# The overflow branch ahead of the last two adds, and the router of blocks 1 to 3 six slots later: fused attention, MLP and top-2 experts on one core

## The chip, the core and the metric

The kernel runs on one core of one Trainium2 chip. TensorE (PE) multiplies matrices and loads its weights on a parallel track (PEld in the profile); VectorE (DVE), ScalarE (ACT) and GpSimd (POOL) do elementwise work, and SyncE (SP) issues transfers. Each engine runs its own queue of instructions in order and waits on semaphores for the others. The metric is the device time of one execution in microseconds (us): a median of 935.31 us over 3 runs before the change (934.85 to 935.39).

## The reference

Three stages, float32 in and out, 2304 tokens of 512 numbers:

```python
scores = where(0 <= i - j < 64, q @ k.T / 8, -1e9)        # 4 sequences x 8 heads x 576 x 64
x = softmax(scores) @ v                                   # heads side by side: 2304 x 512
h = x @ w_in                                              # 512 -> 2048
x = (h * sigmoid(1.702 * h)) @ w_out                      # 2048 -> 512
noisy = x @ w_gate + log1p(exp(x @ w_noise)) * noise      # 8 experts
top2, weights = the two largest of noisy, softmax over the two
out[token] += weight * (relu(x[token] @ w1[e]) @ w2[e])   # for each of its two experts e
```

## The kernel before

Precision: each float32 operand is held as two float16 parts, and each product is three matmuls (high by high, high by low, low by high). So an elementwise result leaves PSUM (TensorE's accumulator memory) as a high part and a low part, made on ACT, DVE and POOL.

Tokens go in 18 tiles of 128 rows, three tiles to a block, blocks 0 to 5. Attention is done tile by tile. The dense MLP is done block by block in 28 slots: 16 slots of its first product (`s1mm`, line 665, twelve matmuls of 384 columns each) and 12 of its second (`s2mm`, line 700, twelve matmuls of 512 columns each, four slots for each tile). After each first product, ACT takes a tanh (line 670), DVE multiplies (line 673, which also frees the PSUM buffer; there are two buffers `h` and two `y`), ACT rounds to the high part (line 676) and POOL subtracts for the low part (line 679). While block c goes through its MLP, the attention of block c+1 runs between the slots: scores on PE (line 486), mask and maximum on DVE (552, 554), exponentials on ACT (560), normalisation on DVE (564 to 570), split on ACT and POOL (578, 581), a transposing transfer issued by SP (586), and the product with v on PE (line 621).

The router picks the experts of a block. Its inputs are the block's MLP rows `R`, transposed by a transfer (`x2t`) and multiplied by the gate weights (`logits`, lines 748 to 751). Nine pieces follow, `route_a` to `route_i`, some 45 small DVE instructions of 3 to 48 columns, a few on ACT, and three small matmuls (`route_g`, lines 823 to 825) that count how many earlier tokens chose each expert. `route_e` (789 to 799) finds the two best experts, `route_f` (804 to 817) makes one-hot masks, `route_h` (833 to 843) the weights, `route_i` (850 to 865) the slot of each token in its expert's list. Then six scatters (`scatter`, line 877, indirect transfers issued by POOL) write token numbers and weights into those lists in DRAM (`xmeta`). The router of block c runs during the MLP of block c+1; that of block 5 runs during the first expert's work.

Each expert's list has 640 places, five row blocks of 128: `gather` fetches rows, `e_stage1` (line 922) and `e_stage2` (line 929) do the two products, and `fin` (lines 948 to 955) scales the rows by their weights on DVE (line 949) and adds them into `out` with an indirect, accumulating transfer issued by POOL (line 952). Empty places carry weight 0 and an output row of their own past the real rows: `NDUMMY` = 128 such rows, shared by all row blocks. What 640 places can't hold is computed by an overflow loop (`overflow_loop`, line 968 on) that goes over all experts and all rows when there is an overflow, and zero times otherwise. Each engine loads the loop's count from memory (`TENSOR_LOAD cti`) and branches.

The order of work: up to the start of block 2's MLP it is a written list (`SEQ`). From there `tasks` holds (time, function) pairs, where time counts slots; before each slot's own matmuls every task that is due is issued. On DVE, ACT, POOL and SP the instructions stand in the order in which they are issued; PE's order is made from it by a scheduler, which can move a group of matmuls past its neighbours. The times of the router, with t0 = 28 (c + 1), the start of the next block's MLP:

```python
for fn, dt, dl in ((route_a, 5, 3.1), ..., (route_e, 10, 3.5), (route_f, 11, 3.6),
                   (route_g, 13, 5), (route_h, 13, 5.2), (route_i, 14, 5.1)):
    at(t0 + (dl if last else dt + ...), fn, c)
at(t0 + (5.4 if last else (15 if c else ...) + 2 * j + a), scatter, c, j, a)
```

`dl` holds for block 5 alone. So `route_e` to `route_i` of blocks 1 to 3 stand in slots 10 to 14, inside the next block's first product; those of block 0 are in `SEQ`.

Of the kernel before, what the change touches and what calls it, by code (L numbers as in the profile page):

```python
# [8 lines left out]
F32 = mybir.dt.float32  # L9
F16 = mybir.dt.float16  # L10
BF16 = mybir.dt.bfloat16
I32 = mybir.dt.int32
# [3 lines left out]
ALU = mybir.AluOpType  # L16
# [6 lines left out]
E, FE = 8, 1024  # L23
NTILE = 18
NCH = 6
CAP = 640
CAPA = 384
MR = 16
NDUMMY = 128
FS = 16  # L30
SL = 28
ET = mybir.EngineType
# [65 lines left out]
def fused_kernel(ctx, tc, q, k, v, w_in, w_out, w_gate, w_noise, noise, w1, w2, out, cap=CAP):  # L98
# [10 lines left out]
    def T(pool, shape, dt, tag, bufs=None):  # L109
        return pool.tile(shape, dt, name=tag, tag=tag, bufs=bufs)  # L110
# [49 lines left out]
    WL = {}  # L160
    WS = {}
    wide = w_in.dtype == I64

    def w_tile(key):
        a = wp.tile([128, 2, 4096], F16, name="w", tag="w", bufs=4)
        WS[key] = (a.rearrange("p s (c n) -> p s c n", c=4), a.rearrange("p s (c n) -> p s c n", c=8))
# [478 lines left out]
    def flush():  # L645
        todo = list(pend)
        pend.clear()
        for fn in todo:
            fn()

    def later(fn):
        pend.append(fn)
# [229 lines left out]
        SC.append(s)  # L882


    XE, ME, OP, ADD = {}, {}, {}, {}
    p2 = {}

    def open2():
# [27 lines left out]
    def moe1(w, x, n, f, o, pool_p):  # L916
        HB[0] += 1
        hp = T(pm, [128, n], F32, "y" if HB[0] > 12 and HB[0] % 2 else "h", 2)
        m = 0
        for d in range(4):  # L920
            for a, s in ((0, 0), (0, 4), (1, 0)):
                pe.matmul(hp, w[:, a, d, 128 * f:128 * f + 128], x[:, s + d, :], start=m == 0, stop=m == 11)  # L922
                m += 1
        later(lambda: relu_split(o, hp))

    def moe2(w, lhs, half, yp):
        for f in range(4 * half, 4 * half + 4):
            for a, s in ((0, 0), (0, 1), (1, 0)):
                pe.matmul(yp, lhs[:, f, a, :], w[:, s, f, :], start=f == 0 and a + s == 0, stop=f == 7 and a == 1)  # L929
# [5 lines left out]
    def e_stage2(e, t, half):  # L935
        part, tt = (0, t) if t < 3 else (1, t - 3)
        g = (gA if part == 0 else gB)[:, :, :, 128 * tt:128 * tt + 128]
        if half == 0:
            OP[e, t] = T(p2["p"], [128, 512], F32, "o", 3)
        yp = OP[e, t]  # L940
        moe2(WS["e2", e][1], g, half, yp)
        if half == 1:
            m = ME[e, part]
            wcol = m[:, tt, e:e + 1].bitcast(F32)
            ids = m[:, tt, 8:9]
            ot = T(p2["s"], [128, 512], F32, "ot", 4)

            def fin():
                dve.tensor_scalar(ot, yp, wcol, None, op0=ALU.mult)  # L949
                if ADD.setdefault(e, []):  # L950
                    pool.memset(C["sp"], 0.0)
                s = pool.indirect_dma_start(out=out, out_offset=bass.IndirectOffsetOnAxis(ap=ids, axis=0),  # L952
                                            in_=ot, in_offset=None, compute_op=ALU.add)
                for o in ADD[e]:
                    tc.declare_no_dep(s.ins, o.ins, reason="an expert takes a token once")
                ADD[e].append(s)
            later(fin)


    def overflow():  # L960
# [7 lines left out]
    def overflow_loop():  # L968
        n = nc.values_load(C["cti"][0:1, 0:1], min_val=0, max_val=E)  # L969
        s2 = p2["s"]  # L970
        with tc.For_i(0, n, 1) as e:
            pool.dma_start(ovd.rearrange("e p t -> p e t"), C["ov"])
            ovc = T(s2, [128, NTILE], F32, "ovc", 1)
            pool.dma_start(ovc, ovd[bass.ds(e, 1)].rearrange("o p t -> p (o t)"))
            for kind in ("e1", "e2"):
                w_tile((kind, "ov"))
                src = (w1 if kind == "e1" else w2)[bass.ds(e, 1)].rearrange("o (c p) f -> p (o c) f", p=128)
                for p in range(4):
                    st = T(mp, [128, 1024], I32, "wst", 3)
                    c = 4 if kind == "e1" else 2  # L980
                    pool.dma_start(st.bitcast(F32).rearrange("p (c n) -> p c n", c=c),
                                   src[:, :, 256 * p:256 * p + 256] if kind == "e1" else src[:, 2 * p:2 * p + 2, :])
                    WL[(kind, "ov"), p] = st
                    wcast((kind, "ov"), p)
            for i in range(NTILE):
                x = T(s2, [128, 8, 128], F16, "xo", 2)
                sp.dma_start_transpose(out=x, in_=x2buf[i + 1])
                ho = T(s2, [128, 8, 2, 128], F16, "ho", 2)
                for f in range(8):
                    moe1(WS["e1", "ov"][0], x, 128, f, ho[:, f], pm)  # L990
                    flush()
                yp = T(p2["p"], [128, 512], F32, "o", 3)
                for half in range(2):
                    moe2(WS["e2", "ov"][1], ho, half, yp)
                ot = T(s2, [128, 512], F32, "ot", 4)
                dve.tensor_scalar(ot, yp, ovc[:, i:i + 1], None, op0=ALU.mult)
                pool.indirect_dma_start(out=out, out_offset=bass.IndirectOffsetOnAxis(ap=C["idm"][:, i, 0:1], axis=0),
                                        in_=ot, in_offset=None, compute_op=ALU.add)


    tasks = []
# [1 line left out]
    def at(t, fn, *a):  # L1003
        tasks.append((t, len(tasks), fn, a))
# [27 lines left out]
    for c in range(NCH):  # L1032
        last = c == NCH - 1
        for j in range(3):
            d = 4 * j if c else 8 + 0.1 * j + P["r0"]
            l = (7 if last and j == 2 else 8) if c else P["l0"]
            at(SL * c + FS + d + (5 if c else P["x0"]), x2t, 3 * c + j)
            at(SL * c + FS + d + l, logits, 3 * c + j)
        t0 = SL * (c + 1)
        for fn, dt, dl in ((route_a, 5, 3.1), (route_b, 6, 3.2), (route_c, 7, 3.3), (route_d, 8, 3.4), (route_e, 10, 3.5),  # L1040
                           (route_f, 11, 3.6), (route_g, 13, 5), (route_h, 13, 5.2), (route_i, 14, 5.1)):
            if last and fn == route_i:
                dl = 5.3
            at(t0 + (dl if last else dt + (0 if c else P["l0"] - 8 + P["r0"])), fn, c)
        for j in range(3):
            for a in range(2):
                at(t0 + (5.4 if last else (15 if c else 17 + P["r0"]) + 2 * j + a), scatter, c, j, a)
    for n in range(4):
        at(2 * SL + 9 + 2 * n, zero_out, n)

# [93 lines left out]
    while ti < len(tasks):  # L1144
        tasks[ti][2](*tasks[ti][3])
        ti += 1
    overflow_loop()


# [27 lines left out]
```

## Time and profile before

| | |
|---|---|
| median of 3 runs | 935.31 us |
| the profiled execution | 933.35 us, of which its span is 931.6 us |
| PE busy | 878.2 us, 94% of the span |
| DVE, ACT, POOL busy | 483.9, 388.2, 372.0 us |
| mean granted TensorE clock | 0.978 of full speed |
| dense MLP of blocks 2 to 5 | 208 to 496 us |
| experts | 497 to 916 us |
| last matmul to end of span | 15.7 us |

The span is from the first to the last instruction. "PE busy" counts matmuls in flight. A row of the timeline has the start in us, the duration (of all that are merged in it), engine, line of the kernel, operation, what it writes and reads, the count (x), and in brackets how long the engine was idle just before and which engine's result, or which transfer, ended that. An engine's name with a q is its sequencer, which handles semaphores, branches and transfer issues and is not counted as busy.

### The profile page before, as it was taken

The numbers are of one execution on the slowest core, as the hardware profiler recorded it, in microseconds if no ns is written. First come the engines' busy times: TensorE is split into PE (matmuls) and PEld (weight loads), VectorE is DVE, ScalarE is ACT, GpSimd is POOL, SyncE is SP. The second block draws the span as 40 slices with busy tenths as digits, with TensorE's granted clock in tenths as the row PEclk, the third lists the DMA queues.
The fourth block names the chain that finished last, engine by engine and source line by source line (L and its number), as shares of the span: only waits on it lengthen the run. The fifth ranks groups of instructions, "written<-read, shape, count | busy, mean of one in ns | idle before, by whom it ended". The sixth has DMA issues, their size and how long they took to land. (4 is left out here: it accounts for less than half of the span.)

```text
span 931.6 us, 16441 instructions
## 1 busy us (share of the span) xinstructions
PE 878.2 (94%) x6355; PEld 502.9 (54%) x6355; DVE 483.9 (52%) x1022; ACT 388.2 (42%) x884; POOL 372.0 (40%) x380
## 2 busy tenths in 40 slices
PE   5898998999899899999999999999999999999993
PEld 4664554545445545545544556674655656474651
DVE  8999976654825734742744522553443525252210
ACT  5888664636426524732633312351322315050200
POOL 2567674826625443551451621432313140323021
PEclk9889999999999999999999999999999999999997
DMA  9899999747887477521248674995866849392112
GB/s 249 215 229 197 232 214 186 129 80 184 238 148 136 81 137 137 81 60 46 91 128 202 142 148 80 231 262 120 192 149 132 209 99 242 48 259 36 23 25 36
DMA packets 255124, 135.90 MB, mean 146 GB/s; under 512 B 207456, under 2 KB 231680, under 8 KB 255040
## 3 DMA queue, kind: packets, MB, share of 16 engines
q1 hardware_dynamic: 218336, 74.28, 41.0%
q0 software_dynamic: 12160, 28.00, 14.3%
q10 hardware_dynamic: 24544, 32.51, 11.4%
q8 instruction: 52, 0.85, 0.4%
q14 instruction: 32, 0.26, 0.1%
HBM read 76.46 MB, written 21.07 MB: 105 GB/s over the span
## 5 line engine op out<-in xcount | busy, mean ns | idle before, releaser
L929 PE MATMUL o<-w,gb 128*128 128x512 f16 x960 | 210.1, 379 | 0.9 <-DVE gb L912 0.7
L700 PE MATMUL y<-w,gb 128*128 128x512 f16 x816 | 185.1, 380 | 0.0
L922 PEld LDWEIGHTS <-w 128*128 128x128 f16 x1536 | 150.1, 98 | 60.5
L952 POOL DMA_INDIRECT out_dram<-ot,me x40 | 69.5, 1739 | 234.7 <-DVE ot L949 228.0
L665 PEld LDWEIGHTS <-w 128*128 128x128 f16 x1152 | 111.5, 99 | 94.1 <-issue 23.1
L929 PEld LDWEIGHTS <-gb 128*128 128x128 f16 x960 | 93.4, 98 | 112.0 <-DVE gb L912 1.6
L665 PE MATMUL h<-xT,w 128*128 128x384 f16 x744 | 137.4, 338 | 14.7 <-DVE gf L673 12.1
L700 PEld LDWEIGHTS <-gb 128*128 128x128 f16 x864 | 82.3, 98 | 94.9 <-issue 1.2
L922 PE MATMUL h<-xe,w 128*128 128x384 f16 (+1 forms) x840 | 126.5, 302 | 0.0
L679 POOL TENSOR_TENSOR gb<-gf,gb 128x384 f16<-128x384 f32 x96 | 91.1, 954 | 81.5 <-ACT gb L676 81.3
L949 DVE TENSOR_SCALAR ot<-o,me 128x512 f32<-128x512 f32 x40 | 30.0, 751 | 144.3 <-PE o L929 122.1
L922 PE MATMUL y<-xe,w 128*128 128x256 f16 (+1 forms) x696 | 102.1, 297 | 0.0
L911 ACT ACTIVATE gb<-y 128x256 f16<-128x256 f32 (+1 forms) x58 | 24.9, 429 | 182.5 <-PE y L922 182.4
L265 DVE SCALAR_TENSOR_TENSOR w<-wst,w 128x1024 f16<-128x1024 f32 x64 | 78.5, 1227 | 40.2 <-ACT w L246 40.2
L246 ACT ACTIVATE w<-wst 128x1024 f16<-128x1024 f32 x64 | 67.5, 1056 | 30.6 <-DVE w L265 17.2
L906 POOL DMA_INDIRECT xg<-x2buf,me x40 | 42.8, 1069 | 72.3 <-DMA me<-xmeta 39.2
L665 PE MATMUL y<-xT,w 128*128 128x384 f16 x408 | 70.0, 326 | 1.5 <-DVE gf L673 1.5
L676 ACT ACTIVATE gb<-gf 128x384 f16<-128x384 f32 x96 | 49.2, 517 | 41.6 <-DVE gf L673 41.6
L560 ACT ACTIVATE sm<-sm,st 128x128 f32<-128x128 f32 x144 | 55.9, 391 | 11.0 <-DVE st L554 10.9
L911 ACT ACTIVATE gb<-h 128x384 f16<-128x384 f32 (+1 forms) x70 | 30.6, 438 | 68.1 <-PE h L922 67.2
L912 DVE SCALAR_TENSOR_TENSOR gb<-h,gb 128x384 f16<-128x384 f32 (+1 forms) x70 | 34.6, 494 | 41.6 <-ACT gb L911 41.6
L877 POOL DMA_INDIRECT xmeta<-rm,slot x36 | 38.5, 1070 | 39.9 <-DVE ov L865 31.5
(167 smaller groups left out, 936.7 us busy)
## 6 DMA issues: line engine op xcount, KB each, us to landing
wst<-in_moe_w_dram ACTq DMA_DIRECT2D x62, 512.0 KB, 4.1
wst<-in_moe_w_in_dram SPq DMA_DIRECT2D x16, 512.0 KB, 4.8
wst<-in_moe_w_out_dram SPq DMA_DIRECT2D x16, 512.0 KB, 4.3
vv<-in_v_dram SPq DMA_DIRECT2D x18, 256.0 KB, 4.8
x2buf<-R SPq DMA_DIRECT2D x18, 256.0 KB, 2.4
kq<-in_k_dram SPq DMA_DIRECT2D x16, 256.0 KB, 4.5
kq<-in_q_dram SPq DMA_DIRECT2D x16, 256.0 KB, 4.5
out_dram<-z POOLq DMA_DIRECT2D x3, 1280.0 KB, 6.2
```

The lines of the kernel that those rows point to most:

```text
L246: act.activation(o[:, 0], i, AF.Copy, scale=s)
L265: dve.scalar_tensor_tensor(o[:, 1], i, s, o[:, 0], op0=ALU.mult, op1=ALU.subtract)
L560: act.activation(sm[:, u, :], sm[:, u, :], AF.Exp, bias=st[:, 0, u:u + 1], accum_out=st[:, 1, u:u + 1])
L665: pe.matmul(hp, w[:, a, d, fs], xt[:, x + d, :], start=n == 0, stop=n == 11)
L676: act.activation(g1[:, f, 0], GF[c, f], AF.Copy)
L679: pool.tensor_tensor(g1[:, f, 1], GF.pop((c, f)), g1[:, f, 0], op=ALU.subtract)
L700: pe.matmul(YP[i], g1[:, f, a, 128 * j:128 * j + 128], w[:, s, f % 8, :], start=f == 0 and a + s == 0, stop=f == 15 and a == 1)
L906: pool.indirect_dma_start(out=xg, out_offset=None, in_=src, in_offset=bass.IndirectOffsetOnAxis(ap=ME[e, part][:, t, 9:10], axis=0))
L911: act.activation(o[:, 0], hp, AF.Relu)
L922: pe.matmul(hp, w[:, a, d, 128 * f:128 * f + 128], x[:, s + d, :], start=m == 0, stop=m == 11)
L929: pe.matmul(yp, lhs[:, f, a, :], w[:, s, f, :], start=f == 0 and a + s == 0, stop=f == 7 and a == 1)
L952: s = pool.indirect_dma_start(out=out, out_offset=bass.IndirectOffsetOnAxis(ap=ids, axis=0), in_=ot, in_offset=None, compute_op=ALU.add)
```

## The change

Four edits:

1. `route_e` to `route_i` and the scatters of blocks 1 to 3 come six slots later: slots 16 to 20 and 21 to 26, inside the second product of the next block's MLP. `route_a` to `route_d` keep slots 5 to 8. Block 4 keeps its times; block 0 is in the written list.
2. For block 5, the third tile's `logits` and all of the router and the scatters come one slot later.
3. The overflow loop stands inside a branch (`tc.If(n != 0)`), and the `fin` of the last expert's row blocks 3 and 4 (two DVE multiplications and two adds of POOL) is issued after that branch, where before all `fin` came ahead of the loop. The loop's result tiles are others (`r`, `xg`), since those of the experts are still held.
4. `NDUMMY` is 1024, so that the empty places of an expert's last two row blocks have output rows of their own. `out` grows by 896 rows, which the kernel neither clears nor returns.

```diff
-NDUMMY = 128
+NDUMMY = 1024
...
-            later(fin)
+            if e == E - 1 and t > 2:
+                LAST.append(fin)
+            else:
+                later(fin)
...
-        with tc.For_i(0, n, 1) as e:
-            pool.dma_start(ovd.rearrange("e p t -> p e t"), C["ov"])
+        with tc.If(n != 0, preferred_fallthrough_block=False):
+            with tc.For_i(0, n, 1) as e:
+                pool.dma_start(ovd.rearrange("e p t -> p e t"), C["ov"])
...
-                yp = T(p2["p"], [128, 512], F32, "o", 3)
+                    yp = T(pm, [128, 512], F32, "r", 1)
...
-                ot = T(s2, [128, 512], F32, "ot", 4)
+                    ot = T(s2, [128, 512], F32, "xg", 4)
...
-            l = (7 if last and j == 2 else 8) if c else P["l0"]
+            l = 8 if c else P["l0"]
...
-        for fn, dt, dl in ((route_a, 5, 3.1), (route_b, 6, 3.2), (route_c, 7, 3.3), (route_d, 8, 3.4), (route_e, 10, 3.5),
-                           (route_f, 11, 3.6), (route_g, 13, 5), (route_h, 13, 5.2), (route_i, 14, 5.1)):
+        late = 0 if last or c == NCH - 2 else 6
+        for fn, dt, dl in ((route_a, 5, 4.1), (route_b, 6, 4.2), (route_c, 7, 4.3), (route_d, 8, 4.4),
+                           (route_e, 10 + late, 4.5), (route_f, 11 + late, 4.6), (route_g, 13 + late, 6),
+                           (route_h, 13 + late, 6.2), (route_i, 14 + late, 6.3)):
...
-                at(t0 + (5.4 if last else (15 if c else 17 + P["r0"]) + 2 * j + a), scatter, c, j, a)
+                at(t0 + (6.4 if last else (15 + late if c else 17 + P["r0"]) + 2 * j + a), scatter, c, j, a)
...
     overflow_loop()
+    for fn in LAST:
+        fn()
```

How the instructions stand, in three places. First DVE during the MLP of block 3, where the weights of block 2's tokens are made (`route_h`). Before:

```order
L570 TENSOR_TENSOR sm<-sm,st 128x512
L833 TENSOR_SCALAR r_wv<-r_wv 128x3
L834 TENSOR_SCALAR r_wv<-r_wv 128x3
L835 RECIPROCAL r_wv<-r_wv 128x3
L836 TENSOR_TENSOR r_wv<-r_wv 128x3
L838 TENSOR_TENSOR r_G<-r_oh_4415,r_wv 128x24
L839 TENSOR_TENSOR r_tg<-r_oh_4416,r_wv 128x24
L840 TENSOR_TENSOR r_G<-r_G,r_tg 128x24
L842 COPY rm<-r_G 128x3x8
L843 COPY rm<-idm 128x3x8
L673 SCALAR_TENSOR_TENSOR gf<-gf,h 128x384
```

The same nine instructions on DVE in the changed kernel:

```order
L554 TENSOR_REDUCE st<-sm 128x4
L636 SCALAR_TENSOR_TENSOR xT<-x,xT 128x4x128
L833 TENSOR_SCALAR r_wv<-r_wv 128x3
L834 TENSOR_SCALAR r_wv<-r_wv 128x3
L835 RECIPROCAL r_wv<-r_wv 128x3
L836 TENSOR_TENSOR r_wv<-r_wv 128x3
L838 TENSOR_TENSOR r_G<-r_oh_4612,r_wv 128x24
L839 TENSOR_TENSOR r_tg<-r_oh_4613,r_wv 128x24
L840 TENSOR_TENSOR r_G<-r_G,r_tg 128x24
L842 COPY rm<-r_G 128x3x8
L843 COPY rm<-idm 128x3x8
L419 COPY qk_4660<-qk_4660 128x8x64
```

The multiplication of line 673, which frees a PSUM buffer of the first product, stood behind them; now the last of these multiplications is past, and what follows is a copy for the attention (line 419).

Second, PE at the three counting matmuls of block 1's router (`route_g`), as a difference: taken out between the scores (486) and a first product (665),

```order
 L486 LDWEIGHTS qT
 L486 MATMUL s<-kT,qT 64x64
-L823 LDWEIGHTS u
-L823 MATMUL r<-r_M,u 128x24
-L824 LDWEIGHTS u
-L824 MATMUL r<-r_mc,u 128x24
-L825 LDWEIGHTS u
-L825 MATMUL r<-r_mc,u 128x8
 L665 LDWEIGHTS w
 L665 MATMUL h<-xT,w 128x384
```

and now between second products (line 700), so that PE meets their wait there.

Third, POOL at the end of the program; `me_9583` are row blocks 0 to 2 of the last expert, `me_9601` row blocks 3 and 4. Before:

```order
L952 DMA out_dram<-ot,me_9583 2432x512
L951 MEMSET sp 1x1
L952 DMA out_dram<-ot,me_9601 2432x512
L951 MEMSET sp 1x1
L952 DMA out_dram<-ot,me_9601 2432x512
L969 TENSOR_LOAD cti
L971 COMPARE_AND_BRANCH
L971 ISA
L971 UNCONDITIONAL_BRANCH
```

In the changed kernel, up to the branch that skips the loop:

```order
L952 DMA out_dram<-ot,me_9583 3328x512
L972 TENSOR_LOAD cti
L974 COMPARE_AND_BRANCH
L974 ISA
L974 UNCONDITIONAL_BRANCH
```

and behind the loop:

```order
L951 MEMSET sp 1x1
L952 DMA out_dram<-ot,me_9601 3328x512
L951 MEMSET sp 1x1
L952 DMA out_dram<-ot,me_9601 3328x512
L1179 UNCONDITIONAL_BRANCH
L1179 ISA
```

The `ISA` instruction of line 971 (now 974) is the one that the profile calls INC_SWDGE_SEM: on the path that skips the loop, POOL first waits until all its earlier transfers have landed, and then sets the semaphores of its transfers to the values that they would have after the loop. Before, this path ends in a block in which every engine waits for all 25 semaphores, twelve instructions on each, and then in the closing barrier (line 1173). In the changed kernel the path leads to the two adds; behind them SP alone waits for the semaphores, and the closing barrier follows.

## Rows read from the trace of the kernel before

**Rows 1.** The page: span.

```profile
span 931.6 us, 16441 instructions
```

**Rows 2.** PE's waits, 225 to 400 us: us in total, times, longest.

```profile
PE h L665 <- DVE gf L673: 7.3, 4, 2.2
PE r L824 <- DVE r_mc L816: 1.1, 2, 0.8
PE r L823 <- DVE r_M L812: 0.7, 1, 0.7
```

**Rows 3.** Timeline, block 2: start us, us, engine, line, work [idle before, releaser].

```profile
244.64 0.55 DVE L673 SCALAR_TENSOR_TENSOR gf<-gf,h 128x384 f32<-128x384 f32 x1
245.24 3.47 PE L665 MATMUL h<-xT,w 128*128 128x384 f16 x12 [2.08 <-DVE gf L673]
...
251.62 1.70 DVE L564 TENSOR_SCALAR st<-st 128x4 f32<-128x4 f32 x1
```

**Rows 4.** Timeline, block 3, DVE and PE.

```profile
308.63 0.69 DVE L789 TENSOR_TENSOR r_ln<-r_ln,r_d 128x24 f32<-128x24 f32 x1
...
317.13 0.88 DVE L833 TENSOR_SCALAR r_wv<-r_wv 128x3 f32<-128x3 f32 x1
...
319.98 0.55 DVE L673 SCALAR_TENSOR_TENSOR gf<-gf,h 128x384 f32<-128x384 f32 x1
...
320.58 2.11 PE L665 MATMUL h<-xT,w 128*128 128x384 f16 x12 [1.86 <-DVE gf L673]
...
323.33 0.19 DVE L865 SCALAR_TENSOR_TENSOR ov<-r_rs,r_G 128x24 f32<-128x24 f32 x1
```

**Rows 5.** Timeline, block 4, DVE and PE.

```profile
386.19 0.69 DVE L789 TENSOR_TENSOR r_ln<-r_ln,r_d 128x24 f32<-128x24 f32 x1
...
388.45 0.55 DVE L673 SCALAR_TENSOR_TENSOR gf<-gf,h 128x384 f32<-128x384 f32 x1
...
389.05 1.98 PE L665 MATMUL h<-xT,w 128*128 128x384 f16 x6 [2.17 <-DVE gf L673]
```

**Rows 6.** Windows: stretch, us, busy us of engines, PEclk (granted clock), DMA share.

```profile
248.00:284.00 36.00, 36.00 (x286) 17.40 (x285) 12.24 (x24) 12.51 (x35) 16.22 (x14) 0.98 0.75 146
245.80:249.30 3.50, 3.50 (x13) 1.54 (x11) 2.57 (x11) 1.83 (x7) 1.85 (x2) 0.51 1.09 222
389.10:392.60 3.50, 3.50 (x15) 1.59 (x14) 2.91 (x11) 1.94 (x7) 0.91 (x1) 0.51 0.12 28
```

**Rows 7.** Timeline of PE after the end of the dense MLP.

```profile
497.41 0.19 PE L751 MATMUL r<-wr,x2T 128*128 128x32 f16 x1 [1.54 <-DMA x2T<-R]
...
509.70 0.19 PE L823 MATMUL r<-r_M,u 128*128 128x24 f16 x1 [0.46 <-DVE r_M L812]
```

**Rows 8.** Timeline, block 2: softmax weights transposed, then used by PE.

```profile
266.78 2.63 SPq L586 DMA_TRANSPOSE PT<-p  x1
...
277.69 0.28 PE L621 MATMUL x<-PT,va 128*64 128x64 f16 x6
```

**Rows 9.** Timeline of POOL at the end: two adds.

```profile
906.61 1.55 POOL L952 DMA_INDIRECT out_dram<-ot,me  x1 [3.59 <-DVE ot L949]
...
916.97 1.55 POOL L952 DMA_INDIRECT out_dram<-ot,me  x1 [3.59 <-DVEq L971]
```

**Rows 10.** Line 952 from 890 us on: issue to landing, us.

```profile
DMA to landing us min/median/max: 4.7/4.8/4.9
```

**Rows 11.** Line 971 from 915 us: ns min/median/max, first and last start.

```profile
L971 SPq EVENT_SEMAPHORE  x12: 28/28/28, 923.6 to 924.3; - x12
L971 PEldq COMPARE_BRANCH  x2: 193/1935/3677, 916.2 to 924.9; - x2
L971 POOLq INC_SWDGE_SEM  x1: 1496/1496/1496, 922.1 to 922.1; - x1
```

**Rows 12.** Line 1173, POOL's sequencer, same columns.

```profile
L1173 POOLq EVENT_SEMAPHORE  x4: 17/17/17, 930.8 to 931.5; - x4
L1173 POOLq DRAIN  x3: 50/109/5420, 925.3 to 931.3; - x3
```

More of the change, by code (lines that the diff above doesn't have):

```diff
@@ L882, in scatter @@
         SC.append(s)
-    XE, ME, OP, ADD = {}, {}, {}, {}
+    XE, ME, OP, ADD, LAST = {}, {}, {}, {}, []
     p2 = {}
@@ L970, in overflow_loop @@
         s2 = p2["s"]
-        with tc.For_i(0, n, 1) as e:
-            pool.dma_start(ovd.rearrange("e p t -> p e t"), C["ov"])
[L973 to L991, printed above, removed]
-                yp = T(p2["p"], [128, 512], F32, "o", 3)
-                for half in range(2):
-                    moe2(WS["e2", "ov"][1], ho, half, yp)
-                ot = T(s2, [128, 512], F32, "ot", 4)
-                dve.tensor_scalar(ot, yp, ovc[:, i:i + 1], None, op0=ALU.mult)
-                pool.indirect_dma_start(out=out, out_offset=bass.IndirectOffsetOnAxis(ap=C["idm"][:, i, 0:1], axis=0),
-                                        in_=ot, in_offset=None, compute_op=ALU.add)
@@ new lines, in overflow_loop @@
+        with tc.If(n != 0, preferred_fallthrough_block=False):
+            with tc.For_i(0, n, 1) as e:
+                pool.dma_start(ovd.rearrange("e p t -> p e t"), C["ov"])
+                ovc = T(s2, [128, NTILE], F32, "ovc", 1)
+                pool.dma_start(ovc, ovd[bass.ds(e, 1)].rearrange("o p t -> p (o t)"))
+                for kind in ("e1", "e2"):
+                    w_tile((kind, "ov"))
+                    src = (w1 if kind == "e1" else w2)[bass.ds(e, 1)].rearrange("o (c p) f -> p (o c) f", p=128)
+                    for p in range(4):
+                        st = T(mp, [128, 1024], I32, "wst", 3)
+                        c = 4 if kind == "e1" else 2
+                        pool.dma_start(st.bitcast(F32).rearrange("p (c n) -> p c n", c=c),
+                                       src[:, :, 256 * p:256 * p + 256] if kind == "e1" else src[:, 2 * p:2 * p + 2, :])
+                        WL[(kind, "ov"), p] = st
+                        wcast((kind, "ov"), p)
+                for i in range(NTILE):
+                    x = T(s2, [128, 8, 128], F16, "xo", 2)
+                    sp.dma_start_transpose(out=x, in_=x2buf[i + 1])
+                    ho = T(s2, [128, 8, 2, 128], F16, "ho", 2)
+                    for f in range(8):
+                        moe1(WS["e1", "ov"][0], x, 128, f, ho[:, f], pm)
+                        flush()
+                    yp = T(pm, [128, 512], F32, "r", 1)
+                    for half in range(2):
+                        moe2(WS["e2", "ov"][1], ho, half, yp)
+                    ot = T(s2, [128, 512], F32, "xg", 4)
+                    dve.tensor_scalar(ot, yp, ovc[:, i:i + 1], None, op0=ALU.mult)
+                    pool.indirect_dma_start(out=out, out_offset=bass.IndirectOffsetOnAxis(ap=C["idm"][:, i, 0:1], axis=0),
+                                            in_=ot, in_offset=None, compute_op=ALU.add)
@@ L1039, in fused_kernel @@
         t0 = SL * (c + 1)
-        for fn, dt, dl in ((route_a, 5, 3.1), (route_b, 6, 3.2), (route_c, 7, 3.3), (route_d, 8, 3.4), (route_e, 10, 3.5),
-                           (route_f, 11, 3.6), (route_g, 13, 5), (route_h, 13, 5.2), (route_i, 14, 5.1)):
-            if last and fn == route_i:
-                dl = 5.3
+        late = 0 if last or c == NCH - 2 else 6
+        for fn, dt, dl in ((route_a, 5, 4.1), (route_b, 6, 4.2), (route_c, 7, 4.3), (route_d, 8, 4.4),
+                           (route_e, 10 + late, 4.5), (route_f, 11 + late, 4.6), (route_g, 13 + late, 6),
+                           (route_h, 13 + late, 6.2), (route_i, 14 + late, 6.3)):
             at(t0 + (dl if last else dt + (0 if c else P["l0"] - 8 + P["r0"])), fn, c)
```

## Prediction, made before the changed kernel was run

> **What bounds the kernel now.** I read the page first: the span is 931.6 us [rows 1], and PE is busy for 94% of it, so time is to be had only where PE stands still, where its clock is halved, and after its last matmul. The view of PE's waits says where it stands still. From 225 to 400 us, the stretch in which the routers of blocks 1 to 3 run, it names three lines and no other: 7.3 us in four waits of a first product for the DVE multiplication of line 673, and 1.1 and 0.7 us of the router's counting matmuls for DVE [rows 2]. The timeline then shows what DVE did instead. In block 3's MLP `route_h` holds DVE from 317.13 to 319.98 us; only then comes line 673, and PE, which had been idle for 1.86 us, goes on at 320.58 [rows 4]. In block 4's MLP `route_e` does the same from 386.19 to 388.45 us, and PE waits 2.17 us [rows 5]. In block 2's it is 2.08 us [rows 3].
>
> The windows show a second cost. In the 3.5 us behind the waits of 2.08 and 2.17 us the granted clock is 0.51, the lower of its two levels [rows 6]: twelve matmuls took 3.47 us [rows 3], where after the wait of 1.86 us, with no such drop, the same twelve took 2.11 us [rows 4].
>
> The tail is read from the lines of the sequencers. The last add is issued at 916.97 us [rows 9] and lands 4.8 us later [rows 10], at 921.8. INC_SWDGE_SEM starts at 922.1 and takes 1.5 us; the other engines pass their twelve waits from 923.6 to 924.3 us [rows 11]. POOL's first DRAIN starts at 925.3 and takes 5.42 us, to 930.7; the barrier behind it runs from 930.8 to the end at 931.6 [rows 12].
>
> **Router, slots 16 to 20.** Nothing is removed; the same instructions move. Ahead of line 673 they go away, and with them the four waits: in block 3 the multiplication would start at 317.13 instead of 319.98, 0.6 us before PE came to want it (320.58 − 1.86 = 318.72, less its 0.55 us); in block 4 at 386.19 instead of 388.45, with PE ready at 386.88. Gain 7.3 us. The counting matmuls leave the first product too: 1.8 us more. Without the two waits over 2 us I expect no clock drop: 2 × 3.5 × (1 − 0.51) = 3.4 us.
>
> What covers the moved work is the second product: from 248 to 284 us PE is busy all 36 us, while DVE is busy for 12.24 us and POOL for 16.22 [rows 6]. The moved DVE work of a block is at most the stretch from its first to its last instruction, 308.63 to 323.52 us, that is 14.9 us [rows 4] with other work in between; 12.24 + 14.9 = 27.1 still fits in 36. `route_f` is issued two slots ahead of the counting matmuls, some 5 us, which must hold a multiplication, the normalisation, and `route_f`. That is tight, so PE may wait for it again: between nothing and the 1.8 us of before [rows 2]. I take 1.0. POOL's six scatters go past its low-part subtractions (679) to stand between the attention's (581, 408); their waits there end with `route_i`, and what they delay is the transpose of the softmax weights. That is issued by SP at 266.78 us and used at 277.69 [rows 8], so 10.9 us less the landing are free. I cost it at nothing.
>
> A rule speaks against the move. DVE's `L564`, four columns, took 1.70 us in the second product [rows 3], where the router's own small instructions take 0.19 [rows 4]. The Trainium skill, "SBUF — State Buffer", section "SBUF: two separate sides", says that some DVE instructions and GpSimd's share a port pair under an exclusive lock, so that whichever comes later waits for the other's whole instruction. By that rule each block could lose 1.70 − 0.19 = 1.5 us ahead of the counting matmuls and the sum below would be 13.5 − 3 × 1.5 = 9.0 us. The trace agrees that such a hold occurs, with that one row; I leave it at the 1.0, because in the changed order POOL's scatters stand behind `route_i`, not beside `L564`.
>
> **Block 5, one slot later.** The third tile's `logits` waited 1.54 us for its transposed rows, the counting matmul 0.46 us [rows 7]. One slot is twelve matmuls, 2.11 us [rows 4], more than either. Gain 2.0 us; between 0 and 2.0, since the whole chain behind moves along.
>
> Sum of the router: 7.3 + 1.8 + 3.4 + 2.0 − 1.0 = 13.5 us. Bounds: 14.5 with no new wait; 7.3 if the clock still drops twice, block 5 gains nothing and PE waits as long as before for the counting matmuls.
>
> **Overflow branch.** What stays: the last add is bound by PE's last matmul and DVE's multiplication, so 916.97 and its landing at 921.8 stand, if POOL is free by then. POOL now waits for row block 2's add (issued at 906.61, landed 4.8 later at 911.4), spends 0.3 + 1.5 us up to 913.2 on what it spent on from 921.8 to 923.6 before, and has 3.7 us left for the add of row block 3 (1.55 us). PE's branch past the loop took 3.68 us [rows 11], from 916.2 to 919.9, off the path as before. What goes: INC_SWDGE_SEM and the waits of all engines behind the last landing. What is late next: SP has 921.8 + 0.7 us for its twelve waits = 922.5. POOL goes from its last add (916.97 + 1.55 = 918.5) into the DRAIN. How long that takes there no row shows: the three of this trace took 5.42, 0.11 and 0.05 us [rows 12]. With 0.05 the end is SP's 922.5 + 0.9 = 923.4; with 5.42 it is 918.6 + 5.4 + 0.9 = 924.9. I take the long one, since it is the first DRAIN in both. Gain 931.6 − 924.9 = 6.7 us; with the short one 8.2.
>
> `NDUMMY` and the other result tiles of the loop cost nothing: the same instructions with other addresses, in a loop that is skipped.
>
> Together 13.5 + 6.7 = 20.2 us: 933.35 − 20.2 = 913.1 us against the profiled execution. The median lies 1.96 us above that execution, so I predict 935.31 − 20.2 = 915.1 us.
>
> **Rivals.**
>
> *POOL is held behind INC_SWDGE_SEM.* Before, POOL stood still until 930.7, which is 8.6 us after INC_SWDGE_SEM began [rows 11, 12]. If that instruction is the cause, it now falls in front of two adds: 911.7 + 8.6 = 920.3 before the first, some 922.0 for the second, landing at 926.8, end at 926.8 + 0.7 + 0.9 = 928.4. The tail gains 3.2 instead of 6.7: 918.6 us. For it: all POOL work was over by then, and two later DRAINs were short. Against it: the other engines saw the new values 1.5 us after it began. The Trainium skill, "GPSIMD Engine Reference", section "Instruction dispatch", has it that the first call to a freshly loaded routine costs about 6 us of loading that no profile instruction shows; the trace's 5.42 us would fit that, and it would hold an add as it held the DRAIN.
>
> *The tail is tied to the last add.* If the DRAIN ends a fixed time after the last add (930.7 − 916.97 = 13.8 us), or the branch keeps a wait for all engines behind the adds, the tail gains nothing: 935.31 − 13.5 = 921.8 us.
>
> *The waits move along.* The router is as much in PE's way in the second product, waits and clock together; what remains is block 5's 2.0 and the tail's 6.7: 935.31 − 8.7 = 926.6 us. Against it stands DVE's 12.24 of 36 us.
>
> *Slower: the softmax chain.* Router work that stands ahead of mask and normalisation makes the transposed weights late for PE. The free time is 10.9 us [rows 8] less a landing of some 3 us (an estimate after the 2.63 us that SP spent on this issue), so about 8 us. To end above 937.2 us the chain must take back 13.5 + 6.7 and 1.9 more, 22.1 us, or 7.4 in each of three blocks. So it decides at 8 + 7.4 = 15.4 us of delay in a block, and the moved work is 14.9 us at most [rows 4]. At 16 us of delay it would be 935.31 − 20.2 + 3 × 8 = 939.1 us.
>
> *It does not do what it says.* The waits move along and the tail is tied as well: 935.31 − 2.0 + 1.0 = 934.3 us.
>
> **How the numbers follow.** The forecast has a chance of 0.60, POOL held 0.20, the tied tail 0.06, the moved waits 0.06, no change 0.04, slower 0.04. The forecast's own range is 912 (no new wait, short DRAIN: 935.31 − 14.5 − 8.2 = 912.6) to 921 (935.31 − 7.3 − 6.7 = 921.3). With POOL held (918.6) and the tied tail (921.8) the range is 911 to 922, which leaves out the last three and the edges. This kernel's runs tell a change from none at about 0.2%, 1.9 us. Faster 0.92, within 0.2% 0.04, slower 0.04.
>
> **What would show it.** Right: no row of PE waiting for line 673 between 225 and 400 us; PEclk at full from 240 to 400 us; router rows on DVE beside line 700 on PE; INC_SWDGE_SEM near 911.7 − 13.5 us; the last landing and the end of the span 3 us apart. Wrong: PE waits for line 823 or 621 in the second product; the two last adds close together and late behind INC_SWDGE_SEM; a DRAIN that ends 13.8 us after the last add.

## The result, and the profile of the changed kernel

| | median us | single times | ratio to before (95%) |
|---|---|---|---|
| before, beside the first measurement | 935.08 | 934.58 to 935.39 (4) | |
| changed kernel | 918.34 | 915.74 to 920.96 (4) | 0.9832 (0.9814 to 0.9850) |
| changed kernel, measured again | 917.06 | 914.04 to 920.40 (6) | 0.9809 (0.9780 to 0.9837) |

The change makes the kernel 16.7 and 17.4 us faster. 20.2 were forecast; both medians lie inside the range, 3.2 and 2.0 us above the predicted 915.1. The profiled execution took 920.96 us, the longest of its four, so single differences between it and the trace of before must be read with care. Its span, against [rows 1]:

```profile
span 919.2 us, 16386 instructions
```

PE's waits from 215 to 500 us, a longer stretch than [rows 2] has (what waited, what for: us, times, longest):

```profile
PE r L751 <- DMA x2T<-R: 2.9, 2, 2.2
PE x L621 <- DMA PT<-p: 1.5, 1, 1.5
```

The waits for line 673 and those of the counting matmuls are gone. What stands there instead is two lines on transfers: one of 2.2 us for the transposed rows at the end of the dense MLP (0.67 us of the 2.9 is an older wait at 215 us), and a new one for transposed softmax weights.

The timeline of block 2's MLP, which answers to [rows 3], shows why the counting matmuls no longer wait:

```profile
246.38 2.75 PE L700 MATMUL y<-w,gb 128*128 128x512 f16 x12
...
251.74 0.17 DVE L817 COPY mrun<-r_mc 128x8 f16<-128x8 f16 x1
...
255.47 0.18 PE L823 MATMUL r<-r_M,u 128*128 128x24 f16 x1
...
261.00 0.19 DVE L865 SCALAR_TENSOR_TENSOR ov<-r_rs,r_G 128x24 f32<-128x24 f32 x1
```

DVE is done with their inputs at 251.9 us, PE comes to them at 255.5; the whole router runs beside line 700. The windows, with the columns of [rows 6], have the clock at full over the three routers, but not everywhere:

```profile
225.00:400.00 175.00, 173.50 (x1551) 96.90 (x1549) 104.15 (x296) 99.22 (x272) 90.73 (x83) 1.00 0.72 141
...
488.90:492.40 3.50, 3.50 (x21) 1.84 (x18) 0.05 (x1) 0.57 (x2) 0.00 (x0) 0.66 0.68 157
...
176.00:179.50 3.50, 3.50 (x33) 2.05 (x33) 0.65 (x2) 1.94 (x4) 0.91 (x1) 0.51 0.98 265
```

Behind the wait of 2.2 us at 486 us the clock drops. It also drops at 176 us, where the two kernels' instructions are still the same. In the trace of before it did not drop there:

```profile
176.00:179.50 3.50, 3.50 (x20) 1.82 (x19) 1.92 (x3) 2.52 (x6) 1.58 (x2) 1.00 1.12 289
```

So this execution was already 2.6 us late at the start of block 2's MLP (210.7 us against 208.1), ahead of everything that the change moves. Over the fourteen traces of this study that start lies between 207.8 and 212.4 us.

The tail, POOL's timeline and then the lines of its sequencer (x count: shortest/median/longest ns, first to last start), against [rows 9], [rows 11] and [rows 12]:

```profile
900.35 1.55 POOL L952 DMA_INDIRECT out_dram<-ot,me  x1 [3.59 <-DVEq L974]
907.50 0.09 POOL L951 MEMSET sp<- 1x1 f32 x1 [5.60 <-DMA out_dram<-ot,me]
908.56 1.55 POOL L952 DMA_INDIRECT out_dram<-ot,me  x1 [0.98 <-issue]
...
910.71 1.55 POOL L952 DMA_INDIRECT out_dram<-ot,me  x1 [0.56 <-DVE ot L949]
```

```profile
L974 POOLq INC_SWDGE_SEM  x1: 1457/1457/1457, 905.5 to 905.5; - x1
...
L1179 POOLq EVENT_SEMAPHORE  x4: 17/17/17, 918.4 to 919.1; - x4
L1179 POOLq DRAIN  x3: 50/115/7880, 910.5 to 918.9; - x3
```

POOL waits for the landing of row block 2's add and passes INC_SWDGE_SEM while PE still multiplies. The first add behind the branch starts 3.1 us after that instruction began. The last add waits for DVE alone. DRAIN ends at 910.47 + 7.88 = 918.35 us, 6.1 after the last add's 1.55. From PE's last matmul (909.6) to the end it is 9.6 us; before it was 15.7. The landing of the last add, in us after its start:

```profile
DMA to landing us min/median/max: 5.1/5.1/5.1
```

So it landed at 915.8, and DRAIN, which POOL came to before that, ended 2.6 us after the landing.

### The profile page after: what moved, and what is told of

It is laid out like the page before. It is cut to its first block, busy times and chain, and to the rows that moved or that the text cites. A ratio compares the mean times of both kernels' runs of the same rounds, so it can differ in the third digit from the quotient of the medians.

```text
span 919.2 us, 16386 instructions
## 1 busy us (share of the span) xinstructions
PE 878.1 (96%) x6355; PEld 503.1 (55%) x6355; DVE 479.4 (52%) x1022; ACT 387.4 (42%) x884; POOL 371.7 (40%) x380
## 5 line engine op out<-in xcount | busy, mean ns | idle before, releaser
L952 POOL DMA_INDIRECT out_dram<-ot,me x40 | 69.4, 1735 | 223.8 <-DVE ot L949 218.4
L665 PE MATMUL h<-xT,w 128*128 128x384 f16 x744 | 135.3, 335 | 7.4 <-DVE gf L673 4.7
```

The costliest lines, as they stand in the source:

```text
L665: pe.matmul(hp, w[:, a, d, fs], xt[:, x + d, :], start=n == 0, stop=n == 11)
```

## The experiments

The forecast says: 11.5 us from blocks 1 to 3, 2.0 from block 5, 6.7 from the tail. The theory that the profile after suggests: about 10 to 12 from blocks 1 to 3, nothing from block 5, because the wait there was read wrongly, and 6.1 from the tail. The rival for the difference between forecast and result is the recorded one, POOL held behind INC_SWDGE_SEM, whose 918.6 us fits the first median best of all cases.

### The three parts alone, and the whole again

**Router of blocks 1 to 3 alone.**

```diff
 (before)
+        late = 0 if last or c == NCH - 2 else 6
-... (route_e, 10, 3.5), (route_f, 11, 3.6), (route_g, 13, 5), ...
+... (route_e, 10 + late, 3.5), (route_f, 11 + late, 3.6), (route_g, 13 + late, 5), ...
```

> The kernel before with one edit alone: route_e to route_i and the scatters of blocks 1 to 3 six slots later. Prediction's step: 7.3 (waits for line 673) + 1.8 (counting matmuls) + 3.4 (two clock drops) - 1.0 (new wait) = 11.5 us, so about 923.6 us against 935.1; no wait of PE for line 673 between 225 and 400 us. Second theory, from the changed kernel's profile: blocks 2 to 4 became 8.4 + 3.6 = 12.0 us shorter there, with no new wait of the counting matmuls but one of 1.5 us for the transposed softmax weights; then 923.1 us, and that 1.5 us wait stands here too if it is what was hidden behind the wait for line 673. Rival: the waits move along (the counting matmuls wait in the second product): 933 us.

924.37 us (923.59 to 925.95) against 934.48; ratio 0.9894 (0.9873 to 0.9915), 7.9 to 11.9 us. PE's waits from 225 to 515 us:

```profile
PE x L621 <- DMA PT<-p: 2.0, 1, 2.0
PE r L751 <- DMA x2T<-R: 1.3, 1, 1.3
PE r L823 <- DVE r_M L812: 0.5, 1, 0.5
```

The second theory holds, wait for softmax weights included. Behind that wait of 1.96 us the granted clock was the lower level for a while, in this trace and not in that of the changed kernel, where the wait was 1.50 us:

```profile
383.50:387.00 3.50, 3.42 (x35) 1.89 (x36) 2.47 (x5) 2.85 (x9) 3.08 (x4) 0.64 0.01 2
```

**Block 5 alone.**

```diff
 (before)
-            l = (7 if last and j == 2 else 8) if c else P["l0"]
+            l = 8 if c else P["l0"]
-... (route_a, 5, 3.1), ...   and the rest of block 5's times
+... (route_a, 5, 4.1), ...   and the rest, one slot later
```

> The kernel before with one edit alone: the third tile's logits, the router and the scatters of block 5 one slot later. Prediction's step: 1.54 + 0.46 = 2.0 us gained, 933.1 us. Second theory: the wait of 1.54 us is that of the second tile's logits, which the edit does not move; its transposing transfer stands on SP behind the three transposes of gathered rows. Then the wait stays between 1.5 and 2.3 us, only the 0.46 us of the counting matmul goes, and the time is 934.6 us (within 0.2% of before), or up to 1.7 us above that if the clock drops behind the wait.

933.67 us (931.03 to 937.34) against 934.48, ratio 0.9994 (0.9975 to 1.0013): no difference that can be told, and the wait of line 751 is still there:

```profile
PE r L751 <- DMA x2T<-R: 1.9, 1, 1.9
```

Its 0.5 us of line 823 behind 509 us is gone. The trace of before shows whose wait it is (SP's queue, ACT and PE around 497 us):

```profile
489.57 4.45 SPq L908 DMA_TRANSPOSE xe<-xg  x3
494.11 1.37 SPq L737 DMA_TRANSPOSE x2T<-R  x1
495.90 0.60 ACT L705 ACTIVATE R<-y 128x512 f16<-128x512 f32 x1 [9.96 <-PE y L700]
497.25 1.24 SPq L737 DMA_TRANSPOSE x2T<-R  x1
497.41 0.19 PE L751 MATMUL r<-wr,x2T 128*128 128x32 f16 x1 [1.54 <-DMA x2T<-R]
```

The third tile's rows leave PSUM at 495.90 us and their transfer is only being issued when PE goes on at 497.41. So PE had waited for the second tile, whose transfer stood on SP behind three transposes of gathered rows until 494.11. The change does not touch the second tile's logits. (That wait was 1.3, 1.5 and 1.8 us in the three traces without this edit, and 1.7 to 2.3 us in the eight that have it and leave the gathers and block 4's scatters alone; whether the edit lengthens it is open.)

**The branch alone.**

```diff
 (changed kernel)
-        late = 0 if last or c == NCH - 2 else 6
 ...   all times of logits, router and scatters as before
```

> The kernel before with the branch around the overflow loop, the last expert's last two adds behind it, the loop's other tiles and NDUMMY 1024, but the router's times as before. Prediction's step: the tail gains 6.7 us (924.9 instead of 931.6), so 928.4 us against 935.1. The changed kernel's profile has 9.6 us from the last matmul to the end where before had 15.7: 6.1 us, 929.0 us. Rival, POOL held behind INC_SWDGE_SEM: 3.2 us, 931.9. Rival, tail tied to the last add: 935.1.

928.85 us (927.22 to 932.04) against 934.48, ratio 0.9934 (0.9912 to 0.9955): 4.2 to 8.2 us. In the trace 9.2 us pass from the last matmul (921.2) to the end (930.4). POOL's timeline there:

```profile
919.75 1.55 POOL L952 DMA_INDIRECT out_dram<-ot,me  x1 [0.98 <-issue]
920.73 0.61 POOL L951 MEMSET sp<- 1x1 f32 x1
922.26 1.55 POOL L952 DMA_INDIRECT out_dram<-ot,me  x1 [0.92 <-DVE ot L949]
```

The last add is again released by DVE: POOL is not held, and the 3.2 us of that rival lie outside the interval. The medians of the three parts lie 10.1, 0.8 and 5.6 us below before, together 16.5; the whole, measured beside them, 17.4. The parts add up.

**The changed kernel again.**

> The changed kernel once more, for a second trace and more times. If the 2.6 us by which its profiled execution was later than before's already at the start of block 2, the 1.7 us of halved clock behind the wait at 486 us and the 1.5 us wait for transposed softmax weights in block 4 belong to the kernel, the median is 918 us and the trace shows the same three losses at the same places. If they are chance (when a transfer lands, and whether the clock drops behind a wait of about 2 us), single times spread from 914 to 921 us and this trace shows other ones.

917.06 us (914.04 to 920.40). The wait for softmax weights (1.78 us) and that of line 751 (1.88 us) are there again, so they belong to the kernel; the clock stayed at full behind both, so that drop differs from run to run. Block 2's MLP started at 210.1 us, again 2.1 us later than in the trace of before, this time without the drop at 176 us. How much of the spread of single times it makes is open.

### The tail

**No overflow loop.**

```diff
 (changed kernel)
-    overflow_loop()
```

> The changed kernel without the overflow loop, its branch and its count's loads (what an overflow would need is left out; with these inputs the loop runs zero times). Theory: all that the branch costs is now beside other work, and the end is set by POOL's DRAIN behind the last add; the time is that of the changed kernel within 1 us, and DRAIN again ends about 7.6 us after the last add's start. Rival: INC_SWDGE_SEM, the branch or the code that PE fetches past the loop (3.9 us) still holds the last adds or the DRAIN; then this is 2 us or more faster.

917.78 us (915.21 to 921.30), the same as with the branch; 8.9 us from the last matmul to the end, against 9.6 and 9.8 in the two traces of the changed kernel. The landing of the last add (start 907.59 us) and the DRAIN:

```profile
DMA to landing us min/median/max: 4.4/4.4/4.4
L1178 POOLq DRAIN  x3: 46/103/7260, 907.4 to 915.1; - x3
```

DRAIN ends at 914.6, 7.0 us after the last add's start and again 2.6 after its landing at 912.0. The add landed 4.4 us after its start here, 5.1 and 5.2 in the changed kernel's traces: this is nearly all of the difference. So the branch costs next to nothing where it stands.

**Only one add behind the branch.**

```diff
 (changed kernel)
-            if e == E - 1 and t > 2:
+            if e == E - 1 and t > 3:
```

> The changed kernel with only the last add behind the branch (t > 3 instead of t > 2), so that POOL waits for the landing of row block 3's add before it. That add starts at 908.6 - 3.2 in the changed kernel's trace at the earliest, at DVE's result (905.3 us), and lands 4.9 us later, at 910.2; then INC_SWDGE_SEM 1.5, branch, memset and waits up to the add 1.6, so the last add starts at 913.3 instead of 910.7 and the end is 2.6 us later. Rival, POOL held 8.6 us behind the start of INC_SWDGE_SEM: last add at 918.9, 8 us later. Rival, the end is not tied to the last add's start: no change.

922.69 us (920.53 to 925.94). POOL's timeline and its INC_SWDGE_SEM:

```profile
907.80 1.55 POOL L952 DMA_INDIRECT out_dram<-ot,me  x1 [3.59 <-DVEq L974]
914.81 0.09 POOL L951 MEMSET sp<- 1x1 f32 x1 [5.46 <-DMA out_dram<-ot,me]
915.87 1.55 POOL L952 DMA_INDIRECT out_dram<-ot,me  x1 [0.98 <-issue]
```

```profile
L974 POOLq INC_SWDGE_SEM  x1: 1477/1477/1477, 912.8 to 912.8; - x1
```

The last add starts 3.1 us after INC_SWDGE_SEM again, not 8.6, and now that is on the path: 12.1 us from the last matmul to the end, 2.6 more than in the changed kernel's first trace, as expected. (The median is 4 to 6 us up. In this trace a wait of 2.3 us at 618 us, a clock drop behind it and one in block 4 are in the same sum; whether that was so in its other runs is open.)

**A memset that waits for the last add.**

```diff
 (changed kernel)
     for fn in LAST:
-        fn()
+        ot = fn()                          # fin now returns its tile
+    pool.memset(ot[0:1, 0:1], 0.0)
```

> The changed kernel with one POOL memset of one element of the last add's source behind that add, so that POOL waits for its landing (6.0 us after its start in the trace) before it comes to the DRAIN. Theory, the DRAIN takes 5.4 to 6.1 us from when POOL comes to it: it begins at about 917 and ends at 922.5 to 923, the end is 4 us later. Rival, the DRAIN ends a fixed 7.6 us after the last add's start, or shortly after its landing: it ends at 918.4 as before and the time is the same within 0.5 us.

920.66 us (918.14 to 920.89), 2.3 and 3.6 us above the changed kernel. POOL's timeline and the DRAIN:

```profile
907.99 1.55 POOL L952 DMA_INDIRECT out_dram<-ot,me  x1 [0.83 <-DVE ot L949]
912.76 0.09 POOL L1155 MEMSET ot<- 1x1 f32 x1 [3.22 <-DMA out_dram<-ot,me]
```

```profile
L1181 POOLq DRAIN  x3: 50/115/5552, 912.7 to 918.9; - x3
```

POOL had nothing to do for 3.2 us and the add had landed, yet DRAIN took 5.55 us from then, as it took 5.42 in [rows 12]. So when nothing is in flight it takes about 5.5 us from when POOL comes to it. That is half of the story. In the six traces with an add in flight that show its landing (the changed kernel twice, the branch alone, no loop, one add, the gathers of the next section), DRAIN ended 2.59 us after the landing each time, while the landing came 4.4 to 5.2 us after the add's start. There the rival's second half holds: the end is tied to the landing. (The tail grew by 2.7 us in this trace, not 4: the forecast took the landing at 6.0 us, and it came after 4.7.)

**NDUMMY as before.**

```diff
 (changed kernel)
-NDUMMY = 1024
+NDUMMY = 128
```

> The changed kernel with NDUMMY 128 as before, so that the empty places of all row blocks share 128 output rows again. Prediction's step: the same instructions with other addresses, no difference: 917 to 918 us, as the changed kernel in its two measurements. Rival: adds of one expert that meet on the same rows are slower; then the landing of the last adds is later than the 4.8 to 5.4 us of the other traces, and the time 1 us or more longer.

916.99 us (914.74 to 924.74), where the changed kernel had 918.34 and 917.06: no cost and no gain that can be told, as the prediction had it. Its trace does not hold the landing of the last adds; its way from the last matmul to the end, 9.0 us, is the shortest of the eight with both adds behind the branch, which speaks against slower adds.

### The waits that are left

**Gathers behind the second tile's transposing transfer.**

```diff
 (changed kernel)
-            at(t0 + (15 if e > 1 else 1) + 0.5 * t, gather, e, 0, t)
+            at(t0 + (15 if e > 1 else 3.1 if e == 0 else 1) + 0.5 * t, gather, e, 0, t)
```

> The changed kernel with the three gathers of the first expert two slots later in the order, so that on SP the transposing transfer of the second tile of block 5 stands ahead of their three transposes. Theory, SP's queue: that transfer is issued at 477.2 instead of 485.5 us, PE no longer waits 2.25 us for it at the end of the dense MLP, nor does the clock drop there (1.7 us): 2 to 4 us faster, and no wait of line 751 near 486 us. Rival, hidden anyway: the gathered rows land at about 488.5 us whatever stands ahead, so the first expert's product waits for them instead, and the time is the same within 0.5 us.

915.95 us (914.44 to 921.41). The rival is right about the trace:

```profile
476.11 1.24 SPq L737 DMA_TRANSPOSE x2T<-R  x1
...
480.57 5.54 SPq L908 DMA_TRANSPOSE xe<-xg  x3
...
488.03 7.69 PE L922 MATMUL h<-xe,w 128*128 128x384 f16 x36 [2.56 <-DMA xe<-xg]
```

Line 751 waits no more, and the expert's first product waits 2.56 us instead, with 36 matmuls in 7.69 us behind it (6.01 at full clock in the trace of before). At this point PE needs both transfers, the transposed rows for the logits and the gathered rows for the expert's first product, and both come late. The median lies 1.1 and 2.4 us below those of the changed kernel; with single times from 914 to 921 us in each, that is no difference that can be told.

**One product with v a slot later.**

```diff
 (changed kernel)
-            at(s0 + P["pv"], pv, i, g)
+            at(s0 + P["pv"] + (1 if (i, g) == (NTILE - 2, 0) else 0), pv, i, g)
```

> The changed kernel with one product of the softmax weights with v (first half of tile 16, in block 4's MLP) one slot later, behind twelve more matmuls of line 665 on PE. Theory: the wait of 1.0 to 2.0 us for the transposed weights at 382 to 385 us, which stands in all six traces that have the later router, was hidden behind the wait for line 673 and is the transfer's own lateness; twelve matmuls (2.1 us) cover it. Then no wait of line 621 there and 1.5 to 2 us less, 915.5 to 916.5 us. Rival: the transfer's lateness comes back as another wait one slot on (line 665 for line 673, or the second half's product): no difference.

916.92 us (915.04 to 919.39). Of the wait 0.3 us is left. The dense MLP of blocks 2 to 4 took 212.3 us; another wait of 1.0 us at 240 us is in it. In the time that cannot be told from the 916.99 of the kernel measured beside it (NDUMMY 128). PE's waits from 370 to 500 us:

```profile
PE r L751 <- DMA x2T<-R: 1.8, 1, 1.8
PE h L665 <- DVE gf L673: 0.5, 2, 0.3
```

**Block 4's scatters at half a slot, alone and with the product moved.**

```diff
 (changed kernel; then with the edit on pv as well)
-... scatter of block 4 at t0 + 15 + 2 * j + a
+... scatter of block 4 at t0 + 15 + 0.5 * (2 * j + a)
```

> The changed kernel with the six scatters of block 4 at half a slot each instead of one slot. Theory: the first expert's gathers wait for the load of its list, and that for the last scatter (started at 468.8 us, landed 6.0 later); with two scatters between two low-part subtractions the last one starts some 2 us earlier, and with it the load, the gathers, their transposes and the second tile's transposing transfer behind them. The wait of line 751 near 486 us falls from about 2 us to under 0.5, and no clock drop follows: 1.5 to 3.5 us less. Rival: POOL's low-part subtractions, now behind two scatters, make PE wait in block 5's second product: no gain, or 1 us more.

> The changed kernel with both edits: the product with v one slot later and the scatters of block 4 at half a slot. If the two waits are independent the gains add: 3 to 5 us less than the changed kernel, 913 to 915 us. Rival: what is gained before the experts is given back at the third expert's gathered rows (a wait of 0.6 to 2.3 us at 616 to 620 us in the traces of the later router), since these come by transfers with their own pace: then 916 to 917 us.

919.86 us (917.96 to 924.63) and 918.69 us (915.98 to 923.82). PE's waits from 370 to 500 us in the first:

```profile
PE y L700 <- POOL gb L679: 2.4, 1, 2.4
PE x L621 <- DMA PT<-p: 1.3, 1, 1.3
```

The wait of line 751 is gone, but the low-part subtractions now stand behind two scatters, and PE waits 2.4 us for one at 466 us (the same in the second kernel). The rival's price was the gain's size. With both edits neither of the two forecasts came true: in that trace blocks 2 to 4 took 211.0 us, the least of all traces, but the wait at 465 us follows, with a clock drop behind it, and none of over 0.9 us at the third expert. No version here is shown to beat the changed kernel; the edits of the gathers and of the product with v were not tried together.

## Why the prediction was right, and where it was not

**Waits for line 673 (7.3 us): right.** The longest left from 225 to 400 us in the traces with the later router is 0.3 us. (One margin was added up wrongly: in block 3 the multiplication at 317.13 would come 318.72 − 0.55 − 317.13 = 1.0 us before PE wants it, not 0.6.)

**Counting matmuls (1.8 gained, 1.0 given back): the second half wrong.** They never wait there; in the changed kernel's first trace DVE was 3.6, 3.5 and 3.0 us ahead of PE in the three blocks.

**What is late next: the wrong wait was named.** In block 4's first product PE now waits 1.0 to 2.0 us for transposed softmax weights, in each of the nine traces with the later router and the product with v unmoved. It is not the softmax chain of the prediction's rival: the transfer was issued at 385.99 us before and, landing 4.2 us later, was 2.6 us ahead of its use at 392.85, behind the wait of 2.17 us [rows 5] and the counting matmuls. Counted from the start of the block's MLP it is issued no later now (28.3 us, before 28.8). With the waits gone PE is there first. Before, and then the changed kernel:

```profile
385.99 1.31 SPq L586 DMA_TRANSPOSE PT<-p  x1
...
392.85 0.28 PE L621 MATMUL x<-PT,va 128*64 128x64 f16 x6
```

```profile
379.74 1.44 SPq L586 DMA_TRANSPOSE PT<-p  x1
...
384.65 0.28 PE L621 MATMUL x<-PT,va 128*64 128x64 f16 x6 [1.50 <-DMA PT<-p]
```

By chance this costs about what I had put down for the counting matmuls.

**Clock (3.4 us): mis-sized.** It held for the profiled execution. But in the trace with block 5's edit alone, whose blocks 2 to 4 are those of before, the wait of 2.08 us stands at 242.8 us and the clock stays at full behind it:

```profile
245.50:249.00 3.50, 3.50 (x21) 1.78 (x19) 2.52 (x11) 1.83 (x7) 1.87 (x2) 1.00 1.10 224
```

So a drop is a possible follower of such a wait, not a certain one, and two of them were no fixed price. From the first matmul of block 2's MLP to that of block 5's, the three traces with the router of before (before, branch alone, block 5 alone) took 224.5, 223.8 and 221.8 us, the nine with the later router and the product with v unmoved 213.1 on the mean (212.4 to 214.6): 10.3 us, where the sum had 11.5. The windows of this stretch, before and changed kernel (the second number is its length, the third PE's busy time; the clock stands behind the engines):

```profile
208.09:432.59 224.50, 214.64 (x1834) 117.44 (x1833) 117.79 (x314) 108.55 (x289) 107.15 (x100) 0.98 0.62 127
...
210.69:423.16 212.47, 210.17 (x1834) 115.99 (x1833) 112.66 (x314) 108.23 (x288) 107.39 (x100) 1.00 0.67 134
```

PE stood still for 9.9 us there, now for 2.3. Over the twelve traces, on the mean, 7.7 of the 10.3 us are standing still (the sum had 7.3 + 1.8 − 1.0 = 8.1) and 1.3 are the clock, of which a drop costs 1.7 us: two before, one with the branch alone, none with block 5 alone, one in two of the nine. The remaining 1.2 us stood in no term: PE was busy that much longer with the same matmuls, drops taken out, when it was stopped more often. Why is open.

**Block 5 (2.0 us): the step that failed.** "The third tile's `logits` waited 1.54 us" was wrong: it was the second tile's. The time at which the third tile's rows left PSUM, 495.90 us, would have shown it. From the first matmul of block 5's MLP to the last of all, the traces took 483.0 to 487.8 us with the edit (both traces of the changed kernel, NDUMMY 128, no loop, one add, memset, block 5 alone) and 483.3 to 485.0 without (before, router alone, branch alone). No gain shows there. What went is the wait of 0.46 us for the counting matmul. With 1.5 us too much this is the largest of the three errors: blocks 2 to 4 gave 1.2 less than forecast, the tail 0.6.

**Tail (6.7 us): right in mechanism, 0.6 us too large.** From 15.7 us (15.4 with the router or block 5 alone) the way from the last matmul to the end came down to 9.0 to 9.8; the sum had 9.0. DRAIN is what is late next, as assumed, but its term was taken from a trace with nothing in flight: it ended 5.5 to 6.2 us behind the last add's 1.55 instead of 5.42, because with the add in flight its end follows the landing by 2.59 us.

**POOL held: refuted,** though its 918.6 us fits the first median best. The time alone would have confirmed a wrong story. The add follows INC_SWDGE_SEM after 3.1 us, not 8.6, and taking the whole loop away gains nothing. The about 6 us of code loading at the first call of a freshly loaded routine that the Trainium skill, "GPSIMD Engine Reference", section "Instruction dispatch", describes would fit the 5.5 us of DRAIN; no run here shows what those are made of, and no add behind the branch was held for such a time.

**The port lock: the holds are real, and cost nothing here.** The 1.70 us of line 564 stand at that place in all three traces with the router of before and in none of the eleven with the later one. But `route_f`'s instruction of line 812, 0.18 us in all three blocks before, now takes 1.10 us in each of the three blocks, ahead of the counting matmuls. In the changed kernel's first trace it ends at 251.03, just behind a subtraction of POOL that ends at 250.99. Below it, from the trace of before, is the subtraction behind which the 1.70 us of [rows 3] ended:

```profile
249.84 1.15 POOL L581 TENSOR_TENSOR p<-sm,p 128x512 f16<-128x512 f32 x1
249.93 1.10 DVE L812 TENSOR_TENSOR r_M<-r_oh,r_oh 128x24 f16<-128x24 f32 x1
```

```profile
252.35 0.94 POOL L679 TENSOR_TENSOR gb<-gf,gb 128x384 f16<-128x384 f32 x1
```

They ended at 253.32, 0.03 us behind this subtraction of line 679 and not with a scatter; the prediction's reason, the place of the scatters, is not what these rows show. The hold costs nothing because of the 3.0 to 3.6 us of room. The Trainium skill, "SBUF — State Buffer", section "SBUF: two separate sides", has DVE and GpSimd share a port pair under an exclusive lock; these rows agree with it. (The prediction's 0.19 us for the router's small instructions was also not the whole of [rows 4], which has 0.69 and 0.88 us for two of them.)

With the steps corrected: 10.3 + 0.5 (line 823 in block 5) + 6.1 = 16.9 us, where 16.7 and 17.4 were measured.

## What to carry to other kernels

A wait that the profile puts down to a transfer names a buffer, and a buffer is written many times: before moving the consumer, find the issue of that very transfer and the evacuation of the data that it carries. When a stall goes, ask of each operand used in the next slots how long it had been ready; those ready for less than the stall's length are the next waits. And when two mechanisms predict nearly the same time, read the trace for the instruction that tells them apart before believing the number.

## What the runs showed of the hardware

POOL's first DRAIN at the end of the program took 5.42 us after waits and 5.55 behind a memset, with nothing in flight. With an add still running it ended 2.59 us after the add's landing, in all six traces that show the landing, and so 5.5 to 6.2 us after the add's 1.55 us. In each of these tails only the closing barrier comes behind it. Behind the memset, which kept POOL from it until the landing, it ended 5.6 us after the landing: coming to it earlier was worth 3 us.

The same wait drops the clock in one execution and not in another: 2.08 us in block 2 with 0.51 behind it [rows 6], and the same 2.08 us with 1.00; the wait for softmax weights with 1.00 at 1.50 and 1.78 us, and with 0.64 at 1.96. Between 225 and 500 us the fourteen traces have thirteen waits of PE of 1.90 to 2.56 us, and behind nine of them the clock dropped. The length alone does not decide it: at 176 us, ahead of all that the edits move, it dropped behind waits of 1.60 and 1.71 us and not behind 1.77 and 2.02. What does stays open.
